# Handing out the slot count of the first expert group in small steps, and issuing the routing exponential with the ranks

## The chip, the core and the metric

The kernel runs on one core of one Trainium2 chip. The metric is the time of one execution on the device in microseconds (us), the median of several runs. The engines of the core are named as in the profile: PE is the matrix engine TensorE, PEld its weight loads, DVE is VectorE, ACT is ScalarE, POOL is GpSimd and SP is SyncE, which here only issues DMAs. Each engine works through its own list of instructions in order; semaphores make one list wait for another.

## What is computed

A gated linear attention (4 batches, 8 heads, 768 steps, 48 wide) is followed by two mixture-of-experts layers. Each picks one of 8 experts for each of the 3072 tokens; the first drops tokens over a capacity.

```
state = f[t] * state + k[t] v[t]^T ;  y[t] = q[t] state        # attention, f = sigmoid(f_logit)
logits = x @ w_gate ; expert = argmax(logits)                  # twice, with other weights
gate = softmax(logits)[expert]
pos = number of earlier tokens with the same expert            # first layer: kept if pos < capacity
out = gate * relu(x @ w1[expert]) @ w2[expert]
```

## The kernel before

The attention works on 24 tiles of 128 tokens (6 to a batch). It is a software pipeline: in iteration `it` every stage of the tuple `STAGES` runs for tile `it - lag`, in the order of the tuple, and the order in which the code is written is the order in each engine's list. Per iteration PE transposes keys (kp), sums the decays (G), forms outputs (y), scores (sc), updates (kv) and, for the router, transposed rows (xp) and logits (rt). ACT empties kp into KT, makes the two exponentials ee of G, copies rows (xr, xT). DVE bounds the decays (F), masks the scores (SC), multiplies keys and queries with the factors (KQ) and adds the states (S). POOL decays the states, scatters list entries with indirect DMAs (tab) and subtracts one chunk of weights per iteration in many iterations (L1010, w0l and w1l).

The PSUM buffers tie these together: sc and kv share one pair of banks (kv waits until DVE has read sc into SC, the next sc until DVE has read kv into S); kp, G and xp share two banks, so xp needs the bank that ACT's KT empties; the router's `rt` has two banks, each of which serves three tiles in turn.

Routing is done for three tiles at once. When a group's last tile (2, 5, 8, 11, 14, ...) is ready, `g_choose` puts the six small DVE instructions of the choice (lsa, mxa, dla, t1a, m2a, oha, and behind the last the exponential `exa` on ACT) on a list named `small`. `step()`, called once or twice behind each large DVE instruction, takes one from the list; `flush()` takes all. One iteration later `g_rank` flushes and issues the rank matmuls (`place`, L130 to L140), which need `oha`; `g_store` then puts the eleven instructions of `slots` and `sums` on the list (t4a, sea, t6a, sfa, sua, the gate, three additions to the running counts `cum1`).

Once, in iteration 24, `lead(11)` counts how many of the first 12 tiles' tokens the first expert has, so that its first group can start early (`first`, L1588): a matmul on PE sums `cum1` into the bank `rt` of tiles 9 to 11, `skip` is copied from it, four steps (`_skip`) make the number of slots to leave out and add it to `cum1`, and `lim` and `caps` are raised by it. The logits of tile 15, last of the iteration's stages, start a new `rt` in that same bank.

After the loop the last tiles and the first expert group are written out by hand; there, too, `place` follows the choice. Then the expert groups of both layers follow, in which PE computes without long pauses.

Of the kernel before, what the change touches and what calls it, by code (L numbers as in the profile page):

```python
# [15 lines left out]
ALU = mybir.AluOpType  # L16
# [7 lines left out]
E = 8  # L24
# [60 lines left out]
def _route_steps(nc, env, psr, lg, J, Pr, cum, gdst, n, scale=None, valid=None, lim=None):  # L85
# [6 lines left out]
    st = _Bag()  # L92

    v = nc.vector
# [23 lines left out]
    def onehot():  # L118
        oh = st.oh = tl("oh", [E], BF16)
        v.tensor_tensor(out=oh, in0=rev, in1=st.m2.unsqueeze(2).to_broadcast(sh), op=ALU.is_equal)  # L120
        if valid is not None:
            v.tensor_tensor(out=oh, in0=oh, in1=valid.unsqueeze(2).to_broadcast(sh), op=ALU.mult)
        if scale is not None:
            v.tensor_tensor(out=st.dl, in0=st.dl, in1=scale.unsqueeze(2).to_broadcast(sh), op=ALU.mult)
        st.ex = tl("ex", [E])
        nc.scalar.activation(st.ex, st.dl, AF.Exp)

# [26 lines left out]
    def add(j):  # L154
        return lambda: v.tensor_tensor(out=cum[:Pr], in0=cum[:Pr], in1=st.oh[:, j], op=ALU.add)
# [32 lines left out]

    st.choice = [logits, largest, below, tied, winner, onehot]
    st.place = place  # L190
    st.sums = [total, guarded, gate] + [add(j) for j in range(J)]
    st.slots = [over, dropped, own, slot, index]
    st.choose = lambda: run(st.choice)
# [5 lines left out]
def _route(*args, **kw):  # L199
    st = _route_steps(*args, **kw)  # L200
    st.choose()
    st.place()
    st.count()
    st.find()
    return st.su
# [21 lines left out]
    ("warm", 0),  # L227
    ("keys_t", 5),
    ("sums", 3),
    ("g_turn", 10),  # L230
    ("g_choose", 10),
    ("rows_t", 8),
    ("expand", 3),
    ("output_i", 7),
    ("scores", 5),
    ("lead", 13),
    ("g_rank", 11),
    ("g_store", 11),
    ("masked", 5),
# [64 lines left out]
def _attention(tc, env, fn, kq, vn, x1, tab1, early, masks, first, side, after, first_group):  # L304


    nc = tc.nc
    with ExitStack() as ctx:
# [15 lines left out]
        tiles = {}  # L324
# [185 lines left out]
        def rows_t(i):  # L510
            t = tiles[i]
            t.xp = p_2.tile([P, NPAIR, P], F32, name=f"xp{i}", tag="tr")[:, :NCC]
            for cc in range(NCC):
                nc.tensor.transpose(t.xp[:, cc], t.xr[:, i % RG, cc * P : (cc + 1) * P], env.ident)
# [42 lines left out]
        small = []  # L557

        def step():
            if small:  # L560
                small.pop(0)()

        def flush():
            while small:
                step()
# [5 lines left out]
        def g_rank(i):  # L571
            if i % RG == RG - 1:
                flush()
                tiles[i].ro.place()

        def g_store(i):
            if i % RG == RG - 1:
                ro = tiles[i].ro
                for a, b in zip(ro.slots, ro.sums):
                    small.extend((a, b))  # L580
                small.extend(ro.sums[len(ro.slots) :])
# [15 lines left out]

        def lead(i):
            if i == SNAP - 1:
                flush()  # L600
                first(tiles[i].rt[:, 104 : 104 + E])

        def warm(i):
            n = NWARM[i] if i < len(NWARM) else 0
# [26 lines left out]
        n = NTILE - 1  # L631
# [10 lines left out]
        output_i(n - 2)  # L642
        scores(n)
        flush()
        tiles[n - 6].ro.place()
        g_store(n - 6)
        masked(n)
# [16 lines left out]
        g_save(n - 6)  # L664
        logits(n - 2)
        tiles[n - 3].ro.choose()
        rows_t(n - 1)
        turn(0)
        rows_c(n - 1)
# [14 lines left out]
        g_list(n - 4)  # L684
        g_turn(n)
        tiles[n].ro.choose()
        product(1)
        product(2)
        g_save(n - 3)
# [157 lines left out]
def _skip(nc, env, n, sel, cum, early):  # L847


    nc.vector.tensor_scalar(out=n, in0=n, scalar1=-1.0, scalar2=float(early), op0=ALU.mult, op1=ALU.add)  # L850
    nc.vector.tensor_scalar(out=n, in0=n, scalar1=0.0, scalar2=None, op0=ALU.max)
    u = env.cp.tile([P, 1], F32, name=f"skip{early}")
    nc.vector.tensor_tensor(out=u, in0=n, in1=env.p4, op=ALU.subtract)
    nc.vector.tensor_scalar(out=u, in0=u, scalar1=0.0, scalar2=4.0, op0=ALU.max, op1=ALU.min)
    nc.vector.scalar_tensor_tensor(out=cum, in0=sel, scalar=u, in1=cum, op0=ALU.mult, op1=ALU.add)


def _overflow_table(nc, env, ef, cr, bud, n, tb, ni):
# [39 lines left out]
def _emit1(tc, env, g, yT, x2, tab2, key):  # L898

    nc = tc.nc  # L900
# [3 lines left out]
    st = _Bag()  # L904
# [25 lines left out]
    def choose():  # L930
        nc.vector.tensor_copy(out=yr[:Pr, :J, C_TID], in_=g.idx)
        st.ro = _route_steps(
            nc,
            env,
            st.rt[:Pr, 384 : 384 + J * E].rearrange("p (j e) -> p j e", e=E),
            st.lg,
            J,
            Pr,
            env.cum2,
            yr[:Pr, :J, C_GATE],  # L940
            g.n,
            scale=gate,
            valid=g.val,
        )
        st.ro.choose()

    def rank():
        st.ro.place()
# [528 lines left out]
def tile_attention_moe_moe(  # L1477
# [5 lines left out]
    nc = tc.nc  # L1483
    env = _Bag()
# [83 lines left out]
    with ExitStack() as mo:  # L1568
# [6 lines left out]
        g0 = M.G[0]  # L1575
# [9 lines left out]
        early = ExitStack()  # L1585
        sel0 = cs[:, C_SEL : C_SEL + E]

        def first(rt):  # L1588

            nc.tensor.matmul(rt, env.oneb, env.cum1, start=True, stop=True)  # L1590
            nc.vector.tensor_copy(out=env.skip1, in_=rt[:, 0:1])
            _skip(nc, env, env.skip1, sel0, env.cum1, g0.N)
            for t in (env.lim, env.caps):
                nc.vector.scalar_tensor_tensor(out=t, in0=sel0, scalar=env.skip1, in1=t, op0=ALU.mult, op1=ALU.add)

        def side(i):
            if i == 5:
# [198 lines left out]
```

## Time and profile before

| | |
|---|---|
| median of 3 runs | 696.89 us (696.06 to 700.9) |
| the profiled execution | 689.96 us, of which 688.1 us span from the first to the last instruction |
| PE busy | 657.0 us, 95% of the span |
| DVE busy | 401.8 us, 58% |
| ACT busy | 305.0 us, 44% |
| POOL busy | 214.1 us, 31% |
| mean granted clock of PE | 0.986 of full speed |

The profile records one execution. In a timeline a row is: start, length, engine, line of the kernel, operation, out<-in, form, count; in brackets the engine's idle time before it and what ended it. The page's line PEclk gives the granted clock in 40 equal slices of 17.2 us, in tenths.

### The profile page before, as it was taken

To read this page: it belongs to the slowest core of one execution; us is meant where nothing else is said; L and a number is where in the kernel's file an instruction comes from. 1 tells how busy PE (TensorE), PEld (TensorE's weight loads), DVE (VectorE), ACT (ScalarE), POOL (GpSimd) and SP (SyncE) were. 2 spreads that over 40 slices of the span, in tenths; PEclk is the share of its full clock that TensorE was granted. 3 is DMA by queue.
4 is the path that set the end of the run, shared out by engine and by line. 5 is a ranking of instruction groups with operands and counts; after the bars stand their busy time and mean duration, and the time that the engine had idled before them with its cause. 6 is when DMAs were issued, how large, how long until landed. Compare 5 with 4: busy or idle time off the path is not lost.

```text
span 688.1 us, 17651 instructions
## 1 busy us (share of the span) xinstructions
PE 657.0 (95%) x6866; PEld 609.1 (89%) x6868; DVE 401.8 (58%) x1067; ACT 305.0 (44%) x649; POOL 214.1 (31%) x233
## 2 busy tenths in 40 slices
PE   7899879799899999999999999999999999999995
PEld 4788768687898999999999999899998899999994
DVE  4655646665586465857566674466455455565642
ACT  4676646543353434344343442154434344354420
POOL 2133344465251223222140320433342222233111
PEclk9999999899999999999999999999999999999998
DMA  9975886234495435454373620375544444345300
GB/s 216 235 229 158 221 226 138 57 99 117 130 287 172 139 113 149 122 140 144 126 181 108 191 71 0 91 253 159 151 113 146 132 153 130 123 143 165 95 26 20
DMA packets 55599, 97.55 MB, mean 142 GB/s; under 512 B 11724, under 2 KB 25006, under 8 KB 55507
## 3 DMA queue, kind: packets, MB, share of 16 engines
q1 hardware_dynamic: 47827, 80.70, 41.3%
q0 software_dynamic: 7680, 15.64, 8.3%
q8 instruction: 56, 0.92, 0.6%
q14 instruction: 36, 0.29, 0.1%
HBM read 80.54 MB, written 16.60 MB: 141 GB/s over the span
## 4 chain that ended last, share of the span: by engine, by line
PE 87%; DMA 7%; DVE 2%; issue 2%; ACT 1%; POOL 0%; DVEq 0%; ACTq 0%; POOLq 0%
PE hpm L1148 30%; PE ypm L1172 10%; PE ypm L1173 10%; PE ypm L1174 10%; DMA out_dram<-yr,tdm 6%; PE y L490 3%; PE G L378 3%; PE tpm L1124 2%; PE kv L443 2%; PE kp L407 2%; PE y L480 2%; PE tym L910 2%; PE warm L612 2%; PE sc L418 1%; PE tym L985 1%
## 5 line engine op out<-in xcount | busy, mean ns | idle before, releaser
L1172 PE MATMUL ypm<-hhm,w1h 128*128 128x288 f32 (+11 forms) x456 | 153.8, 337 | 1.8 <-DVE hlm L1160 1.8
L1173 PE MATMUL ypm<-hlm,w1h 128*128 128x288 f32 (+11 forms) x456 | 150.3, 330 | 0.0
L1174 PE MATMUL ypm<-hhm,w1l 128*128 128x288 f32 (+11 forms) x456 | 150.2, 329 | 0.0
L1148 PE MATMUL hpm<-xhm,w0h 128*128 128x288 f32 (+11 forms) x432 | 147.4, 342 | 0.0
L1159 ACT ACTIVATE hhm<-hpm 128x288 fp32r<-128x288 f32 (+11 forms) x144 | 69.6, 483 | 169.7 <-PE hpm L1148 167.4
L1148 PE MATMUL hpm<-xhm,w0l 128*128 128x288 f32 (+11 forms) x432 | 143.2, 332 | 0.0
L1160 DVE SCALAR_TENSOR_TENSOR hlm<-hpm,hhm 128x288 fp32r<-128x288 f32 (+11 forms) x144 | 78.0, 542 | 103.0 <-ACT hhm L1159 102.8
L1148 PE MATMUL hpm<-xlm,w0h 128*128 128x288 f32 (+11 forms) x432 | 137.7, 332 | 0.0
L294 POOL DMA_INDIRECT xrm<-x,idcm x64 | 71.8, 1122 | 136.0 <-PE hpm L1148 57.3
L1172 PEld LDWEIGHTS ypm<-hhm,w1h 128*128 128x128 f32 x456 | 85.8, 188 | 4.5 <-DVE hlm L1160 1.9
L1173 PEld LDWEIGHTS ypm<-hlm,w1h 128*128 128x128 f32 x456 | 85.9, 188 | 1.9
L1174 PEld LDWEIGHTS ypm<-hhm,w1l 128*128 128x128 f32 x456 | 85.7, 188 | 2.1
L1148 PEld LDWEIGHTS hpm<-xhm,w0h 128*128 128x128 f32 x432 | 81.3, 188 | 2.4
L1148 PEld LDWEIGHTS hpm<-xhm,w0l 128*128 128x128 f32 x432 | 81.4, 188 | 1.9
L1148 PEld LDWEIGHTS hpm<-xlm,w0h 128*128 128x128 f32 x432 | 80.3, 188 | 2.1
L272 POOL DMA_INDIRECT tab<-pos,sum x30 | 33.4, 1112 | 141.0 <-DVE sum L181 134.6
L272 POOL DMA_INDIRECT out_dram<-yr,tdm x34 | 42.3, 1244 | 89.8 <-DVE yr L986 84.0
L1010 DVE TENSOR_TENSOR w0l<-raw,w0h 128x512 fp32r<-128x512 f32 x90 | 60.3, 686 | 8.7 <-ACT w0h L1009 8.1
L1010 DVE TENSOR_TENSOR w1l<-raw,w1h 128x512 fp32r<-128x512 f32 x90 | 59.6, 687 | 0.6 <-ACT w1h L1009 0.3
L1009 ACT CAST w0h<-raw 128x512 fp32r<-128x512 f32 x96 | 57.3, 617 | 0.5 <-DMA raw<-in_w_dram 0.5
L1009 ACT CAST w1h<-raw 128x512 fp32r<-128x512 f32 x96 | 56.9, 623 | 0.0
L1132 ACT CAST xhm<-tpm 128x336 fp32r<-128x336 f32 (+8 forms) x62 | 24.1, 433 | 66.3 <-PE tpm L1124 66.2
(225 smaller groups left out, 894.1 us busy)
## 6 DMA issues: line engine op xcount, KB each, us to landing
raw<-in_w_dram SPq DMA_DIRECT2D x192, 256.0 KB
X<-in_kq_dram SPq DMA_DIRECT2D x48, 192.0 KB
x<-xr SPq DMA_DIRECT2D x8, 582.0 KB
F<-in_fn_dram SPq DMA_DIRECT2D x24, 192.0 KB
Vn<-in_vn_dram SPq DMA_DIRECT2D x24, 192.0 KB
xrm<-x,idcm POOLq DMA_INDIRECT x64, 4.8
tab<-xfill SPq DMA_DIRECT2D x2, 480.0 KB
x<-yr SPq DMA_DIRECT2D x2, 388.0 KB
```

Source lines behind the costliest of these rows:

```text
L272: ins = tc.nc.gpsimd.indirect_dma_start(out=dst, out_offset=bass.IndirectOffsetOnAxis(ap=idx, axis=0), in_=src, in_offset=None, bounds_che ...
L294: nc.gpsimd.indirect_dma_start(out=dst, out_offset=None, in_=src, in_offset=bass.IndirectOffsetOnAxis(ap=idx, axis=0), bounds_check=bound, ...
L378: nc.tensor.matmul(t.G[:, a], t.L[:, 2 * a : 2 * a + 2].rearrange("p h d -> p (h d)"), env.cs[:, C_INC : C_INC + P], start=True, stop=True,)
L1009: nc.scalar.copy(out=hi, in_=raw)
L1010: eng.tensor_tensor(out=lo, in0=raw, in1=hi.bitcast(F32), op=ALU.subtract)
L1132: nc.scalar.copy(out=g.xh[:, :, s], in_=tp[:, :, :Pr])
L1148: nc.tensor.matmul(hp[:, :N], w[:, c, fs], x[:, c, :N], start=(k == 0), stop=(k == len(parts) - 1))
L1159: nc.scalar.activation(hh[:, :N], hp[:, :N], AF.Relu)
L1160: nc.vector.scalar_tensor_tensor(out=hl[:, :N], in0=hp[:, :N], scalar=0.0, in1=hh[:, :N].bitcast(F32), op0=ALU.max, op1=ALU.subtract)
L1172: nc.tensor.matmul(g.yp[d][:, :N], w2h[:, fc, ds_], hh[:, :N], start=(fc == 0), stop=False)
L1173: nc.tensor.matmul(g.yp[d][:, :N], w2h[:, fc, ds_], hl[:, :N], start=False, stop=False)
L1174: nc.tensor.matmul(g.yp[d][:, :N], w2l[:, fc, ds_], hh[:, :N], start=False, stop=(fc == NFC - 1))
```

## The change

Three things. First, `lead` no longer flushes: `first` issues its matmul and returns its eight DVE instructions, which go on the list `small`; in `STAGES` `lead` moves from behind `scores` to in front of `g_turn`, so these eight stand ahead of the choice of tiles 12 to 14. Second, `step()` takes two from the list while more than eight are on it. Third, the exponential leaves the choice and is a function of its own, `weigh`, issued with the ranks.

```diff
@@ _route_steps
         if scale is not None:
             v.tensor_tensor(out=st.dl, in0=st.dl, in1=scale.unsqueeze(2).to_broadcast(sh), op=ALU.mult)
+
+    def weigh():
         st.ex = tl("ex", [E])
         nc.scalar.activation(st.ex, st.dl, AF.Exp)
...
     st.place = place
+    st.weigh = weigh
@@ STAGES
     ("keys_t", 5),
     ("sums", 3),
+    ("lead", 13),
     ("g_turn", 10),
     ("g_choose", 10),
     ("rows_t", 8),
     ("expand", 3),
     ("output_i", 7),
     ("scores", 5),
-    ("lead", 13),
     ("g_rank", 11),
     ("g_store", 11),
@@ _attention
         def step():
-            if small:
-                small.pop(0)()
+            for _ in range(2 if len(small) > 8 else 1):
+                if small:
+                    small.pop(0)()
...
         def g_rank(i):
             if i % RG == RG - 1:
                 flush()
+                tiles[i].ro.weigh()
                 tiles[i].ro.place()
...
         def lead(i):
             if i == SNAP - 1:
-                flush()
-                first(tiles[i].rt[:, 104 : 104 + E])
+                small.extend(first(tiles[i].rt[:, 104 : 104 + E]))
...
+        tiles[n - 6].ro.weigh()
         tiles[n - 6].ro.place()
...
         tiles[n - 3].ro.choose()
+        tiles[n - 3].ro.weigh()
...
         tiles[n].ro.choose()
+        tiles[n].ro.weigh()
@@ _skip
-    nc.vector.tensor_scalar(out=n, in0=n, scalar1=-1.0, scalar2=float(early), op0=ALU.mult, op1=ALU.add)
...
+    for f in _skip_steps(nc, env, n, sel, cum, early):
+        f()
+
+
+def _skip_steps(nc, env, n, sel, cum, early):
+    v = nc.vector
     u = env.cp.tile([P, 1], F32, name=f"skip{early}")
...
+    return [
+        lambda: v.tensor_scalar(out=n, in0=n, scalar1=-1.0, scalar2=float(early), op0=ALU.mult, op1=ALU.add),
+        lambda: v.tensor_scalar(out=n, in0=n, scalar1=0.0, scalar2=None, op0=ALU.max),
+        lambda: v.tensor_tensor(out=u, in0=n, in1=env.p4, op=ALU.subtract),
+        lambda: v.tensor_scalar(out=u, in0=u, scalar1=0.0, scalar2=4.0, op0=ALU.max, op1=ALU.min),
+        lambda: v.scalar_tensor_tensor(out=cum, in0=sel, scalar=u, in1=cum, op0=ALU.mult, op1=ALU.add),
+    ]
@@ first
             nc.tensor.matmul(rt, env.oneb, env.cum1, start=True, stop=True)
-            nc.vector.tensor_copy(out=env.skip1, in_=rt[:, 0:1])
-            _skip(nc, env, env.skip1, sel0, env.cum1, g0.N)
-            for t in (env.lim, env.caps):
-                nc.vector.scalar_tensor_tensor(out=t, in0=sel0, scalar=env.skip1, in1=t, op0=ALU.mult, op1=ALU.add)
+
+            def more(t):
+                return lambda: nc.vector.scalar_tensor_tensor(
+                    out=t, in0=sel0, scalar=env.skip1, in1=t, op0=ALU.mult, op1=ALU.add
+                )
+
+            return [
+                lambda: nc.vector.tensor_copy(out=env.skip1, in_=rt[:, 0:1]),
+                *_skip_steps(nc, env, env.skip1, sel0, env.cum1, g0.N),
+                more(env.lim),
+                more(env.caps),
+            ]
```

What this moves is shown at three places. The numbers behind the names are buffers and differ between the programs. First DVE's list in iteration 24 of the kernel before, from the last instruction of the choice (its other five stand right ahead of it, behind F) to the state additions of the next iteration:

```order
L120 TENSOR_TENSOR oha_2627<-cs,m2a_2625 128x24
L1591 COPY skip_543<-rt_1870 128x1
L850 TENSOR_SCALAR skip_543<-skip_543 128x1
L851 TENSOR_SCALAR skip_543<-skip_543 128x1
L853 TENSOR_TENSOR skip_2635<-skip_543,p_541 128x1
L854 TENSOR_SCALAR skip_2635<-skip_2635 128x1
L855 SCALAR_TENSOR_TENSOR cum_80<-cs,skip_2635,cum_80 128x8
L1594 SCALAR_TENSOR_TENSOR lim<-cs,skip_543,lim 128x8
L1594 SCALAR_TENSOR_TENSOR caps<-cs,skip_543,caps 128x8
L425 TENSOR_TENSOR SC_2641<-sc_2600,cs 128x512
L399 SCALAR_TENSOR_TENSOR KQ_2643<-ee_2580,X_195 128x1024
L459 TENSOR_TENSOR S_2558<-kv_2678,S_2558 128x192 x2
```

The same stretch of the changed kernel, behind F:

```order
L429 TENSOR_TENSOR SC_2619<-sc_2602,cs 128x512
L1615 COPY skip_543<-rt_1870 128x1
L866 TENSOR_SCALAR skip_543<-skip_543 128x1
L403 SCALAR_TENSOR_TENSOR KQ_2623<-ee_2582,X_195 128x1024
L867 TENSOR_SCALAR skip_543<-skip_543 128x1
L868 TENSOR_TENSOR skip_2574<-skip_543,p_541 128x1
L869 TENSOR_SCALAR skip_2574<-skip_2574 128x1
L870 SCALAR_TENSOR_TENSOR cum_80<-cs,skip_2574,cum_80 128x8
L463 TENSOR_TENSOR S_2558<-kv_2662,S_2558 128x192
L1610 SCALAR_TENSOR_TENSOR lim<-cs,skip_543,lim 128x8
L463 TENSOR_TENSOR S_2558<-kv_2662,S_2558 128x192
L1610 SCALAR_TENSOR_TENSOR caps<-cs,skip_543,caps 128x8
```

SC and KQ moved ahead of most of the eight, the eight now lie between SC and the state additions, and the six of the choice follow behind `caps` in a row, ahead of the next iteration's SC.

On PE in iteration 24, before, from the sums of the decays to the logits of tile 15 (rt with xT):

```order
L378 MATMUL G_2568<-cs,L_199 128x128 x4
L265 MATMUL rt_2258<-cs,lts_2514 128x96 x3
L514 MATMUL xp_2576<-cs,xr_2389 128x128 x3
L490 MATMUL y_2519<-Vn_202,SC_2380 64x48 x16
L418 MATMUL sc_2600<-KQ_2384 64x64 x16
L1590 LDWEIGHTS oneb
L1590 MATMUL rt_1870<-cum_80,oneb 128x8
L259 MATMUL rt_2651<-xT_2499,wg1s 32x128 x3
```

And in the changed kernel:

```order
L382 MATMUL G_2568<-cs,L_199 128x128 x4
L1607 LDWEIGHTS oneb
L1607 MATMUL rt_1870<-cum_80,oneb 128x8
L269 MATMUL rt_2258<-cs,lts_2515 128x96 x3
L518 MATMUL xp_2578<-cs,xr_2392 128x128 x3
L494 MATMUL y_2520<-Vn_202,SC_2380 64x48 x16
L422 MATMUL sc_2602<-KQ_2386 64x64 x16
L263 MATMUL rt_2635<-xT_2500,wg1s 32x128 x3
```

The count's weight load and matmul moved from behind the scores to behind G; all else stands as it did.

On ACT around the exponential of the first group (tiles 0 to 2), before, from the decays' exponential to the copy of the rows:

```order
L368 ACTIVATE En_1113<-F_193 128x384
L369 ACTIVATE L_199<-En_1113 128x8x48
L126 ACTIVATE exa_1161<-dla_1100 128x24
L409 COPY KT_1168<-kp_1163 128x512
L390 ACTIVATE ee_1179<-G_1170 128x512
L391 ACTIVATE ee_1179<-G_1170 128x512
L505 COPY xr_1230<-y_1116 128x2x4x48
```

And in the changed kernel:

```order
L372 ACTIVATE En_1113<-F_193 128x384
L373 ACTIVATE L_199<-En_1113 128x8x48
L413 COPY KT_1166<-kp_1161 128x512
L394 ACTIVATE ee_1177<-G_1168 128x512
L395 ACTIVATE ee_1177<-G_1168 128x512
L128 ACTIVATE exa_1214<-dla_1100 128x24
L509 COPY xr_1233<-y_1116 128x2x4x48
```

`exa` moved from in front of KT to behind the second ee; the same holds for the next three groups, and in the fifth it moved into the next iteration.

## Rows read from the trace of the kernel before

**Rows 1.** Page: granted clock of TensorE by slice; chain of waits by engine

```profile
PEclk9999999899999999999999999999999999999998
...
PE 87%; DMA 7%; DVE 2%; issue 2%; ACT 1%; POOL 0%; DVEq 0%; ACTq 0%; POOLq 0%
```

**Rows 2.** Windows of PE: us, busy (instructions), granted clock, DMA share, GB/s

```profile
125.94:127.30 1.36, 0.00 (x1) 1.00 0.81 32
127.30:128.33 1.03, 1.03 (x38) 1.00 0.44 60
128.33:130.70 2.37, 0.00 (x0) 0.75 0.20 40
130.70:132.00 1.30, 1.30 (x33) 0.50 0.05 3
...
135.00:136.00 1.00, 1.00 (x17) 0.50 0.00 0
136.00:137.85 1.85, 1.85 (x65) 0.91 0.02 6
...
98.98:101.00 2.02, 2.02 (x26) 0.50 0.91 299
```

**Rows 3.** Timeline of PE, 117 to 145 us

```profile
127.30 0.42 PE L259 MATMUL rt<-xT,wg1s 128*32 128x128 f32 x6 [1.36 <-DVE skip L1591]
127.65 0.68 PE L480 MATMUL y<-S,KQ 64*64 64x48 f32 x32
130.70 1.11 PE L443 MATMUL kv<-Vn,KT 64*64 64x48 f32 x32 [2.37 <-DVE SC L425]
...
137.85 0.68 PE L480 MATMUL y<-S,KQ 64*64 64x48 f32 x32
...
141.71 0.65 PE L418 MATMUL sc<-KQ 64*64 64x64 f32 x30
...
142.64 0.68 PE L480 MATMUL y<-S,KQ 64*64 64x48 f32 x32
```

**Rows 4.** Timeline of DVE, 117 to 145 us

```profile
124.84 1.88 DVE L112 SCALAR_TENSOR_TENSOR t1a<-dla,cs 128x24 f32<-128x24 f32 x1
...
127.10 0.14 DVE L1591 COPY skip<-rt 128x1 f32<-128x1 f32 x1
...
128.04 1.73 DVE L855 SCALAR_TENSOR_TENSOR cum<-cs,skip,cum 128x8 bf16<-128x8 f32 x1
...
139.36 0.35 DVE L459 TENSOR_TENSOR S<-kv,S 128x192 f32<-128x192 f32 x1
...
142.44 0.69 DVE L425 TENSOR_TENSOR SC<-sc,cs 128x512 f32<-128x512 f32 x1 [1.67 <-PE sc L418]
143.05 0.17 DVE L152 RECIPROCAL xr<-sea 128x3 f32<-128x3 f32 x1
143.13 1.20 DVE L399 SCALAR_TENSOR_TENSOR KQ<-ee,X 128x1024 f32<-128x1024 f32 x1
```

**Rows 5.** Timeline of POOL, 117 to 145 us

```profile
125.38 1.29 POOL L1010 TENSOR_TENSOR w1l<-raw,w1h 128x512 fp32r<-128x512 f32 x1
...
128.46 1.27 POOL L1010 TENSOR_TENSOR w1l<-raw,w1h 128x512 fp32r<-128x512 f32 x1
```

**Rows 6.** Timelines of ACT, 72 to 79 and 96 to 118 us

```profile
73.36 0.22 ACT L126 ACTIVATE exa<-dla 128x24 f32<-128x24 f32 x1 [1.48 <-DVE dla L108]
...
112.80 0.22 ACT L126 ACTIVATE exa<-dla 128x24 f32<-128x24 f32 x1 [1.42 <-DVE dla L108]
```

**Rows 7.** Timelines of PE, 72 to 79 and 96 to 118 us

```profile
74.11 0.55 PE L514 MATMUL xp<-cs,xr 128*128 128x128 f32 x3 [1.00 <-ACT KT L409]
...
98.98 0.88 PE L443 MATMUL kv<-Vn,KT 64*64 64x48 f32 x20 [2.69 <-issue]
...
113.55 0.55 PE L514 MATMUL xp<-cs,xr 128*128 128x128 f32 x3 [1.00 <-ACT KT L409]
```

**Rows 8.** Timeline of DVE, 72 to 79 us

```profile
72.28 1.04 DVE L108 TENSOR_TENSOR dla<-lsa,mxa 128x24 f32<-128x24 f32 x1
```

More of the change, by code (lines that the diff above doesn't have):

```diff
@@ L201, in _route @@
     st.choose()
+    st.weigh()
     st.place()
@@ L847, in _skip @@
 def _skip(nc, env, n, sel, cum, early):
-    nc.vector.tensor_scalar(out=n, in0=n, scalar1=-1.0, scalar2=float(early), op0=ALU.mult, op1=ALU.add)
-    nc.vector.tensor_scalar(out=n, in0=n, scalar1=0.0, scalar2=None, op0=ALU.max)
+    for f in _skip_steps(nc, env, n, sel, cum, early):
+        f()
+def _skip_steps(nc, env, n, sel, cum, early):
+    v = nc.vector
     u = env.cp.tile([P, 1], F32, name=f"skip{early}")
-    nc.vector.tensor_tensor(out=u, in0=n, in1=env.p4, op=ALU.subtract)
-    nc.vector.tensor_scalar(out=u, in0=u, scalar1=0.0, scalar2=4.0, op0=ALU.max, op1=ALU.min)
-    nc.vector.scalar_tensor_tensor(out=cum, in0=sel, scalar=u, in1=cum, op0=ALU.mult, op1=ALU.add)
+    return [
[5 more added lines that the diff above has]
+    ]
 def _overflow_table(nc, env, ef, cr, bud, n, tb, ni):
@@ L945, in choose @@
         st.ro.choose()
+        st.ro.weigh()
     def rank():
```

## The prediction

> **What bounds the kernel now.** I read the page first: its chain of waits lies on TensorE (PE) for 87% of the span, and the line of granted clock shows PE at full speed except in a few slices, one of them the eighth (120 to 137 us) [rows 1]. So only time in which PE stands still, or runs at its lower clock, can be won. All that the change moves runs inside the attention loop, before about 150 us; later stages only start earlier or later by what the loop gains.
>
> Next I read, in the windows and PE's timeline, the stretch with the loop's only call of `lead` (iteration 24). Two idle pieces of PE stand there. From 125.94 to 127.30 PE does nothing in 1.36 us; the timeline says that the router's logits (L259) wait for `skip`, the copy at L1591. From 128.33 to 130.70 it does nothing in 2.37 us; the updates (kv) wait for the mask product SC on VectorE (DVE) [rows 2, 3]. Then the granted clock is 0.50, the lower of the two levels (1.2 GHz of 2.4), in five windows from 130.70 to 136.00, and 0.91 in the next [rows 2].
>
> DVE's timeline tells why. Before SC stands one run of 14 small instructions: six that choose the expert, then `skip`, `cum`, `lim`, `caps`. Their own work is small (0.14 us for the copy, about 0.19 from one start to the next), but two of them took 1.88 and 1.73 us [rows 4]. Each ended within 0.1 us of the end of a weight subtraction on GpSimd (POOL): those ran 125.38 to 126.67 and 128.46 to 129.73 [rows 5]. So DVE was held, twice, while POOL worked.
>
> Last I read the routing exponential `exa` on ScalarE (ACT) and its neighbours. At 73.36 and 112.80 ACT stood 1.48 and 1.42 us waiting for `dla` from DVE, with the copy KT queued behind it [rows 6]. PE's transposes xp reuse the PSUM buffer that KT empties, and waited 1.00 us for KT both times [rows 7].
>
> **The change, part by part.**
>
> *The lead.* Lost in the profiled run: 1.36 + 2.37 = 3.73 us idle, and at half speed 5.30 × 0.50 + 1.85 × 0.09 = 2.82 us. Together 6.55 us. A second reading agrees for what follows the first wait: from y to y this iteration takes 137.85 − 127.65 = 10.20 us, the next one 142.64 − 137.85 = 4.79, so 5.41 us more, where idle and half speed make 2.37 + 2.82 = 5.19 and the rank matmuls the rest [rows 2, 3].
>
> What stays: the copy of `skip` is now behind SC, and the logits still need it, since their PSUM buffer is free only then. SC starts about 0.08 us after the scores end (142.36, SC at 142.44), the next instruction starts 0.61 later, and the copy takes 0.14, after which the logits followed in 0.06 [rows 3, 4]. So PE waits about 0.9 us there; the bounds are 0.9 and 1.36, what it waited before. The choice is no longer in front of SC, and SC no longer behind `caps`, so the 2.37 goes. I take the half-speed stretch as gone too: the window right after the idle piece of 1.36 us has clock 1.00, and the fall comes only within the piece of 2.37 [rows 2].
>
> What is late next: with the scores' end as zero, DVE runs SC to 0.7, the copy to 0.85, one `skip` step to 1.05, KQ (1.20) to 2.2, four steps of 0.19 to 3.0, two state additions with `lim` and `caps` (2 × 0.36 + 2 × 0.1) to 3.9, and the six of the choice (about 0.2 each) to 5.1 [rows 4]. On PE the next scores end one iteration after the logits start, at 0.9 + 4.79 = 5.7 [rows 3]; right behind them stands the rank matmul, which needs the choice's last output. The slack is 0.6 us. If POOL holds DVE once for the length of a subtraction (1.29), the rank matmul is 0.7 us late; if not, 0. I take 0.5, nearer the upper end, because DVE was held twice in the same stretch before [rows 4, 5]. A rule speaks for the upper end: the Trainium skill ("SBUF — State Buffer", "Who interferes with whom") says that a DVE instruction with two SBUF inputs and a GpSimd instruction that reads SBUF exclude each other, the one that came second waiting out the whole of the first. The trace agrees (1.88 and 1.73 us for instructions of 0.2); taken strictly it makes this loss 0.7 and the gain 0.2 smaller.
>
> The term: 6.55 − 0.9 − 0.5 = 5.15 us. Bounds: 6.55 − 1.36 − 0.7 − 2.82 = 1.67 (the clock falls all the same) to 6.55 − 0.9 = 5.65.
>
> *The exponential.* Issued with the ranks, `exa` stands behind KT and both ee, and `dla` is done by then. KT then starts when its transposes end, and xp has no wait: 2 × 1.00 = 2.0 us. The two other early ranks show no idle of PE in front of xp and give 0. `exa` itself (0.22 us) goes into a place where ACT next waits for PE's y, so costs 0. On DVE the sum `sea` now stands one place ahead of KQ; ACT has finished `exa` by then, and 0.1 us of DVE ahead of KQ delays nobody, since DVE waits 1.67 us for the scores before SC anyway [rows 4, 6, 7]. That `dla` itself is held (1.04 us at 72.28, for work of 0.2) stays as it was [rows 8]; nothing on PE needs it so early. Bounds 1.0 (one of the two was held by something else as well) to 2.9, the waits of ACT itself.
>
> *The double step.* In four ranks the eleven instructions of `slots` and `sums` are handed out sooner: three of them, about 0.1 us each where they lie between others, now stand ahead of the state additions. Two additions of 0.35 us from 139.36 on would end by 140.1 if nothing held DVE, 1.6 us before the next scores at 141.71 [rows 3, 4]; so the cover is 1.6 us and I cost it at nothing; the list's scatters on POOL and the gate column become ready earlier, which nobody waits for on PE in this stretch.
>
> **Sum.** 5.15 + 2.0 = 7.15 us, in the profiled execution 689.96 − 7.15 = 682.8. The runs' median is 696.89, 6.93 us above that execution; the trace cannot say where those 6.93 lie, so I carry them unchanged: 696.89 − 7.15 = 689.7. With the bounds of the terms the gain is 2.7 to 8.55 us, which gives 694.2 to 688.3.
>
> **The rivals.**
>
> *The clock falls all the same.* PE now has idle pieces of 0.9 and perhaps 0.5 us within one iteration instead of 1.36 and 2.37. For it: at 98.98 a single idle piece of 2.69 us was followed by 0.50 as well, so the fall needs no second piece [rows 2, 7]. Against it: the piece of 1.36 left the clock alone. Price 2.82, so 692.6. Chance 0.10.
>
> *POOL holds DVE twice again.* The two holds of 1.88 and 1.73 us come back between KQ and the choice's end: 3.6 us, less 0.6 of slack, makes the rank matmul 3.0 late instead of 0.5. Gain 4.65, 692.2; if that piece also brings the lower clock, as 2.37 did, 695.1. For it: both holds were in this stretch [rows 4, 5]. Against it: the run of small instructions now has KQ and the state additions in it, which read PSUM or wait for PE anyway, so fewer of its instructions meet a subtraction. Chance 0.15.
>
> *The end does not follow.* The loop is shorter but something after it takes the time back, such as the first expert group's gather. Against it: its producers all move with the loop, and the chain stays on PE. Half the gain then, 693.3. Chance 0.05.
>
> *Slower: the double step is held by POOL.* With the small steps bunched behind KQ, the state additions come late in each of the four ranks. One hold of 1.88 us eats the cover of 1.6 and costs 0.3; from two holds on (3.6 us) PE loses 2.0 us in each rank, and above an idle piece of about 2.4 us the lower clock with 2.8 more. Four ranks at 2.0 are 8.0, against the gain of 7.15: 697.7; with two falls of the clock 703.4. It decides where two holds fall into one rank. For it: `dla` was held at 72.28 and would be again [rows 8]. Against it: that was a single hold of 1.04 us; two in one run of instructions stand only in the lead's stretch [rows 4]. Chance 0.06.
>
> *More than I count.* The 6.9 us between profile and median could be further stretches at the lower clock of this kind, and some of those would go with the lead's stall: 687 or less. Chance 0.09.
>
> **How the numbers follow.** The forecast has 0.55. About 1% (7.0 us) is what a measurement of this kernel can tell from no change, and the forecast of 7.15 lies on that bound: about 0.33 of its 0.55 is beyond it and 0.22 short of it, since the half-speed term and the two waits of xp are read off rows and only the 0.5 is a guess. Faster: 0.33 + 0.09 of the last rival + 0.02 for the scatter of the median (three runs from 696.06 to 700.9), 0.44. Slower by over 1% needs the two holds in several ranks and a fall of the clock: 0.05. The rest, 0.51, is within 1%. The range reaches down to 686.0, which takes in the upper bound and part of the case of more, and up to 695.5, which takes in the fall of the clock, the double hold and the end that does not follow; the likeliest case's own range is 688.3 to 691.5.
>
> **What would show it right or wrong.** Right: in iteration 24 PE's logits wait about 0.9 us for the copy of `skip`, kv waits for nothing, no window near 131 to 136 has clock 0.50; `exa` follows ee, ACT does not wait for `dla`, and the two waits of xp for KT are gone. The lead's step is wrong if kv or the rank matmul waits over 1 us, or if the clock falls there. The exponential's step is wrong if xp waits as before, or if DVE waits for `exa`. The sum is wrong if PE's idle pieces marked "issue" in the rows (2.69 us at 98.98) grow or move: I assumed them unchanged [rows 7].

## The result and the profile after

The changed kernel took 700.24 us (median of 13 runs, 696.72 to 705.76), the kernel before beside it 696.29 us (13 runs, 693.26 to 700.9). The ratio is 1.0064 with a 95% interval of 1.0035 to 1.0093: slower by 0.64%. That is within my 1%, but outside my range and on the other side of no change, so the 0.51 that I gave to "within 1%" came true by luck. The profiled execution took 699.45 us.

The page of the changed kernel (TensorE's line of part 1, the granted clock by slice, the chain):

```profile
PE 661.8 (95%) x6868; PEld 613.0 (88%) x6868; DVE 401.5 (58%) x1067; ACT 305.4 (44%) x649; POOL 212.5 (30%) x233
...
PEclk9999999999999999999999999999999999999999
...
PE 83%; DMA 7%; DVE 3%; another core or an unknown queue 2%; issue 2%; ACT 2%; SPq 0%; POOL 0%; ACTq 0%; DVEq 0%; POOLq 0%
```

No slice of the clock lies below 9 any more [rows 1], and yet the span is longer; new in the chain is "another core or an unknown queue". First the forecast's own places. PE's timeline in iteration 24 of the changed kernel (the rows that answer to [rows 3]):

```profile
134.64 0.42 PE L263 MATMUL rt<-xT,wg1s 128*32 128x128 f32 x6 [0.94 <-DVE skip L1615]
134.99 0.68 PE L484 MATMUL y<-S,KQ 64*64 64x48 f32 x32
135.49 0.65 PE L447 MATMUL kv<-Vn,KT 64*64 64x48 f32 x32
...
139.54 0.17 PE L132 MATMUL rt<-oha,trib 128*128 128x24 bf16 x1
```

The logits wait 0.94 us for `skip` (forecast 0.9), kv waits for nothing (2.37 before), the rank matmul of the next iteration follows its scores. So the lead did what it should. The loss shows elsewhere. PE's waits in the loop (14 to 152 us; the columns are total us, times, longest):

```profile
PE y L484 <- issue: 6.0, 14, 1.1
...
PE kv L447 <- DVE SC L429: 1.3, 4, 0.4
...
PE rt L263 <- DVE skip L1615: 0.9, 1, 0.9
```

The series y (queries with states) is interrupted 14 times, 12 of them at four places, three at each. In the first profile of the kernel before no such row stands among PE's waits. The timeline of PE, POOL, DVE and ACT at one of the four:

```profile
84.52 0.65 PE L422 MATMUL sc<-KQ 64*64 64x64 f32 x30
...
84.80 1.04 POOL L276 DMA_INDIRECT tab<-tokid,sua  x1 [0.56 <-issue]
...
85.10 0.42 PE L263 MATMUL rt<-xT,wg1s 128*32 128x128 f32 x6
...
85.45 0.32 PE L484 MATMUL y<-S,KQ 64*64 64x48 f32 x6
...
86.06 0.36 PE L484 MATMUL y<-S,KQ 64*64 64x48 f32 x4 [0.29 <-issue]
...
86.14 0.98 POOL L276 DMA_INDIRECT tab<-tokid,sua  x1 [0.31 <-issue]
86.83 0.35 PE L484 MATMUL y<-S,KQ 64*64 64x48 f32 x6 [0.40 <-issue]
...
87.55 0.50 PE L484 MATMUL y<-S,KQ 64*64 64x48 f32 x16 [0.38 <-issue]
...
87.66 0.69 DVE L429 TENSOR_TENSOR SC<-sc,cs 128x512 f32<-128x512 f32 x1 [4.31 <-remote]
87.74 0.47 ACT L539 COPY lts<-rt 96x384 f32<-96x384 f32 x1 [1.63 <-remote]
```

While POOL issues two scatters (84.80 to 87.12), PE advances by four to six matmuls and then stands 0.3 to 0.4 us, again and again. The scores' rows end at 85.17 by the model of the profile, but SC, which needs only them, starts at 87.66: what PE signals comes late too ("remote" is a wait whose releaser the profile does not find). I call this the hold. The other three places are alike, with SC waiting 2.99, 2.98 and 4.35 us at 67.68, 106.48 and 126.37. The double step is what brought the pair there: `sua`, which the scatters need, is ready earlier, so they start on the scores and y, all 64x64 matmuls, instead of on kv, kp and G; the experiments test that.

### The profile page after: what moved, and what is told of

Read it like the earlier page. It is cut to its first block, busy times and chain, and to the rows that moved or that the text cites. A ratio compares the mean times of both kernels' runs of the same rounds, so it can differ in the third digit from the quotient of the medians.

```text
span 697.6 us, 17653 instructions
## 1 busy us (share of the span) xinstructions
PE 661.8 (95%) x6868; PEld 613.0 (88%) x6868; DVE 401.5 (58%) x1067; ACT 305.4 (44%) x649; POOL 212.5 (30%) x233
## 4 chain that ended last, share of the span: by engine, by line
PE 83%; DMA 7%; DVE 3%; another core or an unknown queue 2%; issue 2%; ACT 2%; SPq 0%; POOL 0%; ACTq 0%; DVEq 0%; POOLq 0%
PE hpm L1165 30%; PE ypm L1189 10%; PE ypm L1190 10%; PE ypm L1191 10%; DMA out_dram<-yr,tdm 6%; PE G L382 3%; PE y L494 2%; PE tpm L1141 2%; PE kv L447 2%; PE kp L411 2%; PE tym L926 2%; PE sc L422 1%; PE y L484 1%; PE tym L1002 1%
```

## The experiments

Times are medians; before was run beside each on the same chip. The result names the chip by number, and the chip turned out to matter. The chip of the first comparison has no number in it.

| run | chip | us | before | ratio (95% interval) |
|---|---|---|---|---|
| lead and exponential, single step | 7 | 689.68 | 691.35 | 0.9968 (0.9931 to 1.0005) |
| double step alone | 7 | 690.12 | 691.35 | 0.9983 (0.9946 to 1.0019) |
| exponential alone | 7 | 692.07 | 691.35 | 0.9999 (0.9961 to 1.0037) |
| lead alone, single step | 7 | 688.87 | 691.35 | 0.9973 (0.9940 to 1.0005) |
| changed kernel again | 13 | 689.36 | 692.60 | 0.9964 (0.9935 to 0.9993) |
| before again | 13 | 691.58 | 692.60 | 1.0001 (0.9977 to 1.0026) |
| single step again | 13 | 687.26 | 692.60 | 0.9943 (0.9917 to 0.9969) |
| double step alone again | 13 | 690.91 | 692.60 | 0.9987 (0.9959 to 1.0015) |
| changed kernel, third time | 5 | 703.79 | 700.23 | 1.0044 (1.0004 to 1.0084) |
| single step, third time | 5 | 698.09 | 700.23 | 0.9971 (0.9936 to 1.0007) |
| changed kernel, fourth time | 14 | 689.27 | 691.32 | 0.9972 (0.9934 to 1.0010) |
| double step for the lead's list alone | 14 | 690.12 | 691.32 | 0.9973 (0.9940 to 1.0007) |
| blocks shifted | 14 | 691.12 | 691.32 | 1.0004 (0.9964 to 1.0044) |

**The parts one by one.** My theory (A): the double step costs, by moving the scatters. The rivals: the exponential or the lead costs (B), or only the tail after the loop (C).

```diff
 def step():                       # single step; the flush acts in iteration 24 alone
-    for _ in range(2 if len(small) > 8 else 1):
-        if small:
-            small.pop(0)()
+    if small:
+        small.pop(0)()
 def lead(i):
     if i == SNAP - 1:
+        flush()
         small.extend(first(tiles[i].rt[:, 104 : 104 + E]))
```

> The changed kernel with step() taking one small instruction at a time again (and a flush ahead of the count's matmul, so that the running count is complete): lead and exponential as changed, double step undone. Theory A (the double step makes the list's scatters ready earlier, so that POOL issues its pair of indirect DMAs while PE runs the 64x64 matmuls of y and the scores, and PE is held there for about 2 us in each of four groups): the pairs start again about 1 us later, on kp, G and kv; the rows y [0.38 <-issue] in series go, DVE's SC no longer waits 3.0 to 4.4 us at 67.7, 87.7, 106.5 and 126.4, and the time is below that of before: 689 to 693 where before has 696. Rival B (the exponential and its sum, or the lead itself, cost the time): as slow as the changed kernel, 699 to 701, with the waits of SC still there. Rival C (the tail alone, 147 to 170 us, is lost by another timing of its gathers): 696 to 698, the loop repaired and the tail as late as in the changed kernel.

> The kernel before with the double step alone. Theory A: the pairs of scatters fall on y and the scores in the first four groups, SC waits 3 us and more there, and the time is 6 to 10 us above before, 702 to 706. Rival B (exponential or lead cost the time): no slower than before, 695 to 697, with SC waiting under 2 us. Rival C (the tail alone): 696 to 700 with no waits of 3 us in the loop.

> The kernel before with the exponential issued with the ranks, alone. Theory A (and my forecast): the two waits of 1.00 us of xp for KT go, about 2 us faster, 693.5 to 695.5. Rival B: 1 to 4 us slower, 697 to 700, by the sum sea that stands ahead of KQ on DVE and is held 1.15 us by POOL's subtraction.

> The kernel before with the lead alone handed out in small steps (single step, flush ahead of the count's matmul), exponential where it was. Theory A (and my forecast): kv no longer waits 2.4 us in iteration 24, no window at the lower clock there, 3 to 5 us faster, 691 to 693.5. Rival B (the lead costs the time): the same or slower, 696 to 700, with the logits or the rank matmul waiting over 1 us in iteration 24 or 25.

None is slower than before, so B falls. But theory A falls as I had put it: the double step alone was not 6 to 10 us slower, though its scatters lie exactly where they lay in the changed kernel. Its timeline (double step alone, chip 7):

```profile
84.53 0.65 PE L418 MATMUL sc<-KQ 64*64 64x64 f32 x30
...
84.79 1.03 POOL L272 DMA_INDIRECT tab<-tokid,sua  x1 [0.56 <-issue]
...
85.46 0.68 PE L480 MATMUL y<-S,KQ 64*64 64x48 f32 x32
85.49 0.69 DVE L425 TENSOR_TENSOR SC<-sc,cs 128x512 f32<-128x512 f32 x1 [3.70 <-PE sc L418]
...
86.13 0.98 POOL L272 DMA_INDIRECT tab<-tokid,sua  x1 [0.30 <-issue]
...
86.24 0.68 PE L443 MATMUL kv<-Vn,KT 64*64 64x48 f32 x32
```

Here y is one series of 32 and kv starts 86.24 − 85.46 = 0.78 us after it; in the first profile of the changed kernel kv started at 88.41, 2.96 us after y's 85.45. Same order at this place, same alignment within 0.02 us, 2.2 us apart. At the other three places kv starts 2.47 to 3.01 us after y in the first profile and 0.73 to 0.85 here, so the hold takes 1.7 to 2.2 us at each. The exponential alone gained nothing (forecast 2.0), the lead 1.9 us by the ratio (forecast 5.15, bounds 1.67 to 5.65), with an interval that takes in no change.

**The same kernels on other chips.** New theories: the hold belongs to the chip or the execution (D), or to the whole program (E).

> The changed kernel once more, unedited, on the same chip as the kernel before, the single step and the double step alone. In the first profile of it PE was held 2 to 2.5 us in four groups while POOL issued a pair of scatters on the 64x64 matmuls; the kernel with the double step alone had the pairs at the same places and PE lost only 0.3 us there. Theory D (the hold is not a property of the order but of the execution or the chip on which it was taken): no hold here, PE's y in one series of 32, about 2 to 4 us faster than before as forecast less what the scatters cost. Theory E (the hold belongs to this program, by the double step together with the other two parts): held again, SC waiting 3 to 4.4 us at 67, 87, 106 and 126 us, 3 to 5 us slower than before.

> The kernel before once more, unedited, for a second profile: theories D and E both expect a ratio of 1 and the same stalls as in the first profile (kv 2.4 us behind SC in iteration 24, two waits of xp of 1.0 us); what differs between the two profiles is the scatter of one execution.

> The changed kernel with the double step undone, again, on the chip of the changed kernel's second run. Theory E (the double step with the other parts is what costs): 4 us and more faster than the changed kernel. Theory D: within 1 us of the changed kernel's second run.

> The kernel before with the double step alone, again. Theory D, if the chip decides: the pairs of scatters hold PE here too if this chip is the one of the first run (SC waiting 3 us and more, slower than before), and not if it isn't. Theory E: as in its first run, no hold, 0 to 1 us below before.

On chip 13 the unedited changed kernel shows no hold and is 0.36% faster than before: D, and E falls. (Theory D had the single step within 1 us of it; it lay 2.1 ahead, with intervals that overlap.) The opposite case came with chip 5, where two more runs had most of the weights' loads cut away:

```diff
+if i < 16:
+    raw, src = raw[:, :64], src[:, :64]      # then repeated 8 times by the split
 self.nc.sync.dma_start(out=raw, in_=src)
```

> The changed kernel unedited, a third time, beside the single step. Theory D (the hold of PE by the scatters belongs to the chip of the first run): if this chip is like the second, no hold and 2 to 3 us faster than before; if like the first, SC waiting 3 us and more at 67, 87, 106 and 126 us and 3 to 5 us slower than before, with the single step then 6 us and more ahead. Theory F alone says nothing of the hold, but has the issue waits at the ends of the same instruction blocks as in the second run.

> The changed kernel with one small instruction at a time, a third time: 2 to 4 us faster than before on any chip (theory A or E: 2 us or more faster than the changed kernel; theory D: 0 to 2 us faster than it on a chip without the hold).

> The kernel before with the first 16 chunks of weights loaded an eighth wide (64 of 512 columns, repeated by the split; the weights' values are left out by that, every instruction on PE, DVE, ACT and POOL stays), so that most of the weights' traffic leaves the attention loop. Theory F (PE's waits marked issue are waits for blocks of its own instruction list, which arrive late behind data on the DMA engines: PE resumes 1.2 to 1.5 us after a packet of queue 8 ends, at the same instruction in each execution): the issue waits of 0.7 us and more after 50 us go or shrink to under 1 us in sum, and the kernel is 2 to 4 us faster than before. Theory G (the issue waits have nothing to do with the traffic): the same waits at the same instructions, ratio 1.

> The changed kernel with the same cut of the weights' loads. Theory F (the stalls that the change takes away come back as late instruction blocks, because PE now reaches a block's end sooner): with the traffic gone no such wait takes their place, and this kernel is 5 to 7 us faster than the kernel before with the same cut. Theory G: 2 to 3 us faster than it, as with the traffic.

On chip 5 the changed kernel is held again and 0.44% slower than before; the single step, on the same chip, is not slower (0.9971). DVE's waits for SC from 60 to 130 us, changed kernel and then single step, both on chip 5:

```profile
DVE SC L429 <- remote: 12.1, 3, 4.3
```

```profile
DVE SC L429 <- PE sc L422: 28.3, 11, 4.0
```

The single step has no row marked remote (its profiled execution took 705.25 us, 7 above its median). Between the two medians lie 703.79 − 698.09 = 5.7 us: this is what the double step costs on this chip. On chip 13, where nothing is held, the same pair differs by 2.1, so not all of the 5.7 need be the hold. The pair with cut loads says the same: DVE's waits from 60 to 130 us, kernel before with the cut,

```profile
DVE SC L425 <- PE sc L418: 22.9, 10, 3.5
```

and changed kernel with the cut, both on chip 5:

```profile
DVE SC L429 <- remote: 16.3, 4, 4.3
DVE SC L429 <- PE sc L422: 15.0, 6, 4.9
```

Four waits of the kind seen first, and none in the order of before in this stretch. (The total time of these two, 745.26 and 751.39 us, is no measure: with weights left out the second layer's tokens go elsewhere and later work differs.) What they say of the traffic comes below.

**Without the scatters.** In `g_list` the scatters of tiles 0 to 13 are left out.

```diff
-_scatter1(tc, "tab1", tab1, t.ro.su[:, k : k + 1], env.tokid[:, n], E * RC - 1)
+if not loop[0]:
+    _scatter1(tc, "tab1", tab1, t.ro.su[:, k : k + 1], env.tokid[:, n], E * RC - 1)
```

> The changed kernel without the scatters of the loop (the list entries of tiles 0 to 13 are left out, so later stages work on other rows and their time is not to be read; only the loop is). Theory D and A (on a chip that holds, POOL's scatters are what holds PE): the series of y with pieces of 0.35 us and idle 0.38 us goes in the first four groups, and DVE's SC does not wait for a late end of the scores, so the loop up to the last kp is 5 to 8 us shorter than in the unedited kernel beside it. On a chip that does not hold: at most 1 us shorter. Rival H (another load of that stretch holds PE, such as the DMAs of X, F and the weights): the pieces stay.

> The changed kernel unedited once more, as the mark of what this chip does: with the hold, 3 to 5 us slower than before and SC waiting 3 us and more at four groups; without, 1 to 4 us faster than before.

> The kernel before without the scatters of the loop (the list entries of tiles 0 to 13 are left out, so the rows that later stages work on are others). Theory I (the scatters also delay the blocks of PE's list, by their own small transfers): a loop of 127 to 129 us from the first kp to the last against 130 to 133 with scatters, the wait for a block near 75 us under 1 us, and 3 us and more faster than before on a chip without the hold. Theory F alone (the blocks are late whatever the scatters do): the same waits for blocks as with scatters, within 1 us of before.

> The changed kernel without the scatters of the loop, in several rounds, on the same chip. Theory I: 4 to 7 us faster than the kernel before without them, which is what I forecast for the change (7.15 us, less about 1 for late blocks), since nothing that the double step moves is left. Theory F alone: 2 to 3 us faster than it, because the waits taken away come back as late blocks; then the look of 681.8 us was the scatter of one execution. On a chip with the hold both would be 8 us and more faster than their kernels with scatters.

The first execution without them was on chip 14, which does not hold: 681.8 us against 689.27 for the unedited kernel, where I had expected a loop at most 1 us shorter. In the two profiles the loop, from the first kp to the last, takes 125.6 and 132.3 us, though PE's waits add up to nearly the same (10.8 and 11.6). The granted clock differs: the lower level holds nowhere in the loop without scatters and for 13.7 us in the other, at half speed 6.8 us. One execution of each cannot say whether the scatters are the cause. The later pair ran on chip 12, where before takes 700.04: without the loop's scatters before takes 691.49 (ratio 0.9892, 0.9854 to 0.9930) and the changed kernel 688.58 (0.9835, 0.9797 to 0.9872). Later stages work on other rows here, but what follows the loop takes 546.2 and 546.6 us, as in the held executions of the changed kernel (545.6 and 548.2), so I compare these totals. The scatters then cost some 8 us even in the order of before on that chip; part of it may be clock, since the lower level holds for 3.4 us of the loop in both profiles and for 10.2 in the two of before on other chips. With the scatters gone the loop shows no hold in either (DVE's waits for SC, changed kernel), while behind the loop, where scatters are left, the same profile has it:

```profile
DVE SC L429 <- PE sc L422: 20.2, 12, 2.8
```

```profile
151.28 0.99 POOL L276 DMA_INDIRECT tab<-tokid,sua  x1 [0.30 <-issue]
...
152.90 0.48 ACT L509 COPY xr<-y 128x384 f32<-128x384 f32 x1 [4.46 <-remote]
```

So the hold goes with the scatters; whether POOL's issuing or the small transfers that it starts is what holds PE was not separated. The change is now worth 691.49 − 688.58 = 2.9 us, nearer the 2 to 3 of theory F (next) than the 4 to 7 of theory I. With six runs each, spread over 4.5 and 5.2 us, that makes it likely, but does not show, that the shortfall is not the scatters' doing.

**The waits marked issue.** Why 2 to 3 us instead of 7 where nothing is held? PE's waits from 14 to 152 us on chip 13, kernel before:

```profile
PE sc L418 <- issue: 2.4, 2, 1.6
PE kv L443 <- DVE SC L425: 2.4, 1, 2.4
PE xp L514 <- ACT KT L409: 1.8, 3, 1.0
PE rt L259 <- DVE skip L1591: 1.4, 1, 1.4
...
PE y L490 <- issue: 0.8, 1, 0.8
```

and the changed kernel:

```profile
PE sc L422 <- issue: 5.4, 3, 3.1
PE G L382 <- issue: 2.4, 1, 2.4
PE kv L447 <- issue: 2.0, 3, 1.2
...
PE rt L263 <- DVE skip L1615: 1.2, 1, 1.2
PE y L484 <- issue: 1.2, 2, 0.9
```

The waits for SC and KT are gone, and "issue" has grown. Summed over all rows of this view, waits on other engines and on issue are 7.5 and 7.5 us in the first profile of before and 8.0 and 4.3 in the second; in the unheld profiles with lead and exponential (changed twice, single step twice, lead's list) they are 3.1 to 4.0 and 8.5 to 12.6. On the mean 4.3 us of named waits went and 4.8 us of issue came. These are single executions: in them the loop is no shorter (131.6 to 135.5 us against 133.4 and 130.5), while by the ratios of the table these kernels lie 0.27 to 0.57% below before, 2 to 4 us. The profiles show where waits went, not the net. What is issue? Queue 8 of the trace carries instructions, in packets of 16 KB. In the unheld profiles the issue waits of 0.4 us and more in the loop end 1.1 to 1.7 us after such a packet has ended; and counted over all of PE's records, matmuls, weight loads and the semaphore instructions between them, nearly all of them stand at number 192 to 195 over a multiple of 256. (My expectation below says matmuls and weight loads, 191 to 193; over those alone the number drifts from 182 down to 142 in the loop.) PE waits for the next block of its own list. The longest one, on PE's timeline of the changed kernel on chip 13:

```profile
76.57 0.47 PE L422 MATMUL sc<-KQ 64*64 64x64 f32 x15
80.11 0.46 PE L422 MATMUL sc<-KQ 64*64 64x64 f32 x15 [3.07 <-issue]
```

The DMA view of the stretch from 77 to 79 us has the packet (packets, MB, share), that of 73 to 77 has none:

```profile
q8 instruction: 1, 0.02, 3.3%
```

It ran from 77.62 to 78.67, and PE went on 1.44 us after its end. In before, on the same chip, the same 15 scores wait 1.65 us, from 74.41 to 76.06, for a packet that ended at 74.70. What follows such a wait, in windows of PE (us, busy of PE, PEld, DVE, ACT, POOL, granted clock, DMA share, GB/s):

```profile
77.04:80.11 3.07, 0.00 (x1) 0.00 (x0) 0.00 (x0) 1.55 (x4) 0.00 (x0) 1.00 1.04 264
...
82.00:84.00 2.00, 2.00 (x18) 1.91 (x16) 1.81 (x10) 0.40 (x1) 0.00 (x0) 0.50 0.23 45
84.00:86.00 2.00, 2.00 (x23) 1.83 (x22) 0.00 (x0) 0.82 (x3) 0.00 (x0) 0.67 0.95 275
```

The clock falls to the lower level there, as it did behind the lead's stall: that price moved with the waits. The test of the blocks: 64 more matmuls with their weight loads at the head of the list.

```diff
-spin(i, n)
+spin(i, n) if i else spin(0, n + 64, 64)     # 75 matmuls of 64 columns for 11 of 512
```

> The changed kernel with single steps and, in the warm-up of iteration 0, 75 matmuls of 64 columns in place of 11 of 512: 64 matmuls and 64 weight loads more on PE's list, ahead of everything that is looked at, and otherwise the same order. In the profiles so far each wait of PE marked issue of 0.4 us and more stands where the count of PE's instructions (matmuls and weight loads) is 191 to 193 over a multiple of 256, 1.2 to 1.7 us after the end of a packet of the instruction queue. Theory F (PE waits for blocks of 256 instructions): the waits leave their places (the scores near 77 us, 15 of the series behind the wait; G near 98; kv near 61, 17 behind it) and stand half a block, some 2 to 2.5 us of work, away from them; counted anew they are at one other residue of 256, 63 to 65. Theory G (the place in the program decides, not the block): the waits stay at the scores, G and kv with the same number of matmuls behind them. The time is not the point of this run; the longer warm-up may cost up to 3 us.

The waits left their places. PE's timeline near 78 us, single step with shifted blocks:

```profile
73.19 0.68 PE L447 MATMUL kv<-Vn,KT 64*64 64x48 f32 x32
78.22 1.01 PE L411 MATMUL kp<-cs,KQ 128*128 128x128 f32 x4 [4.36 <-issue]
```

The scores that follow, two at 82.81 and 30 at 82.91, are no longer split by a wait; it now stands at the kp ahead of them. My count in the expectation was muddled: with the added 128 instructions counted in, the places must stay at 192 to 195 over a multiple of 256, and they do (194 and 195); without them it is 66 and 67. So blocks of the list decide, not the place in the program. Why a block is late was not settled. Its packet starts up to 5.7 us after PE has entered the block ahead, 1.5 to 2.1 on the mean of each profile; with the weights' loads cut to an eighth it is 1.8 and 1.5, and 1.6 in the uncut changed kernel on that chip. The longest wait for a block is 1.2 us in all three. So those bytes do not explain it, and theory F's part on the traffic is not borne out.

**A version meant for both kinds of chip.**

```diff
-for _ in range(2 if len(small) > 8 else 1):
+for _ in range(2 if len(small) > 11 else 1):
```

> The changed kernel with two small instructions at a time only while the list has more than 11, which holds in the lead's stretch alone (and a flush ahead of the count's matmul): the scatters of the first four groups stay where the single step has them. Theory A with D: no hold of SC of 3 us on any chip, 2 to 5 us faster than before, equal to the single step within 1 us, the rank matmul of iteration 25 not waiting (it waited 0.4 to 1.3 us for oha with the single step). If the lead's double step is itself the cost: slower than before.

With no more than 11 entries the list is handed out singly, so the scatters stay. On chip 14 it is level with the changed kernel (690.12 and 689.27); that chip does not hold, so what it would save on one that does was not seen. The single step was seen on both kinds: ahead of the changed kernel by 2.1 us on chip 13 and by 5.7 on chip 5, and ahead of before by 0.29 to 0.57% on three chips, of which one interval excludes 1.

## Why the prediction was wrong

*The double step: the step that failed where a chip holds.* I wrote that the scatters "become ready earlier, which nobody waits for on PE in this stretch", and set 0. Nobody waits for their results, but PE is held while they are issued. In place of 0 the cost is 1.7 to 2.2 us at each of four places in the trace, and 5.7 us net in time on chip 5. My rival for slower had the right edit and the wrong mechanism: it had POOL hold DVE and the state additions late. The Trainium skill ("SBUF — State Buffer", "Who interferes with whom") says that PE and ACT never wait on anyone there. It speaks of SBUF's ports, and which resource is at work here no run shows; that POOL's work cannot slow PE does not follow, as kv 2.96 us behind y, against 0.78, shows.

*Issue assumed unchanged: the step that failed where nothing is held.* I named it as an assumption, with the 2.69 us of [rows 7], and gave it no price. In the profiles without the hold it grew by 4.8 us on the mean, more than the 4.3 us of named waits that went. The Trainium skill ("Runtime: NRT & Kernel Launch", "Instruction fetch mechanics") has the list fetched in blocks of 16 KiB, 256 instructions, by a queue of its own, and calls the cost of a boundary mostly hidden. The block size agrees with the packets and the count; hidden it is not here: nearly all of the 8.5 to 12.6 us of issue, in the 138 us looked at, stand at block ends. With its first half at hand I could have seen that the 2.69 us of before also ended 1.47 us after such a packet.

*The 6.93 us carried from the profiled execution to the median: perhaps a wrong base.* The page that I read came from an execution that shows no hold behind the loop: 539.7 us from the last kp to the end, as in all unheld executions (538.7 to 540.9). In the held ones of the changed kernel this part takes 545.6 (its first profile) and 548.2, 6 to 8 us more, with no edit of the order there. The first profile shows it on PE, POOL and ACT:

```profile
160.06 1.11 PE L494 MATMUL y<-Vn,SC 64*64 64x48 f32 x32
...
160.38 1.07 POOL L276 DMA_INDIRECT tab<-tokid,sua  x1 [3.69 <-DVE cum L157]
...
164.68 0.48 ACT L509 COPY xr<-y 128x384 f32<-128x384 f32 x1 [4.48 <-remote]
...
165.21 0.90 PE L518 MATMUL xp<-cs,xr 128*128 128x128 f32 x3 [3.69 <-ACT xr L509]
```

The kernel before was without a profile on that chip, so that its 696.29 us contain this is an inference, from 700 us on chips 5 and 12, which hold, and 691 to 693 on the three that don't. The difference of 6.93 may then be the trace of a regime that I had not seen; but on chip 13 one profiled execution of before lay nearly as far under its median (685.37 and 691.58) with no such cause, so the scatter of one execution is not excluded.

*The lead: right in mechanism at its place, the term too large.* From the kp of iteration 24 to that two iterations later the two unheld profiles of before take 16.78 and 15.83 us, the unheld changed kernel 11.97 and 11.98: 3.9 to 4.8 us against 5.15. The logits' wait (0.94 in the first profile, 1.2 on chip 13, forecast 0.9) and the free kv are as foreseen. In time the lead alone gave 1.9, with an interval that takes in 0. Where the rest went stays open: the issue waits of its profile are 6.7 us, between the 7.5 and 4.3 of before.

*The exponential: its waits went, its gain did not come.* The two waits of xp [rows 7] are absent wherever it is moved. Alone it gave a ratio of 0.9999: its profile has issue waits of 3.17 us at 77.93 and 2.85 us at 115.75, right behind the two places that were freed, and the lower clock holds for 20.5 us of the loop, against 10.2 in the profiles of before.

*The clock.* It stands at 0.99 from 131 to 136 us of the first profile, as forecast for iteration 24; the rival in which it falls all the same came true elsewhere, behind the hold (0.59 from 127 to 131 us there) and behind the late blocks. Over the whole loop nothing was won: by the granted clock the lower level holds for 10.2 us in both profiles of before, and for 6.8 to 13.7 us (mean 11.6) in the five unheld ones with lead and exponential. So the 2.82 us of half speed in my term left iteration 24 and came back in other places. The 2.4 us of idling that I set for a fall in the rival of the double step does not hold either: on chip 13 the kernel before falls behind the wait of 1.65 us (low from 76.6 on).

## What to carry to other kernels

A wait that is removed is won only up to the next thing that is late: where PE's waits marked issue repeat at one instruction modulo 256, count them as a limit beside the engines, and expect a freed PE to reach it. Before a small list of instructions is handed out faster, look at what its last entry releases: an indirect DMA that POOL issues is work with a place in time, here better off series of short matmuls, where the single step has it (5.7 us on chip 5). If the profiled execution lies 1% under the median, take a second profile before a gain is read off the first. Where a stall that brought the lower clock is removed, add up the time at the lower clock over the whole stage, and not at that place alone.

## What was not expected of the hardware

- The kernel before runs at 691 to 693 us on chips 7, 13 and 14 and at 700 on chips 5 and 12. On chip 5, on that of the first comparison, and on chip 12 behind the loop, PE is held while POOL issues indirect DMAs: on short 64x64 matmuls four to six go out and then 0.3 to 0.4 us pass, and what waits for PE starts up to 3.5 us late (xr at 164.68, for a y that ends at 161.17). What differs between the chips no run shows.
- PE's list arrives in packets of 16 KB for 256 instructions, of 0.9 to 3.0 us each, and where PE waited it goes on 1.1 to 1.7 us after the end of one. A block's work takes 3.5 to 5 us where nothing waits, so little is left for a late start.
